# First softmax of a recurrent attention step done 320 wide, the step's end by halves, and the last step's loads put elsewhere

## The chip, the cores and the metric

The kernel runs on one core of a Trainium2 chip, as one launch. The time is the device time of that launch in microseconds (us). Five runs of the kernel before took 2143.23 to 2150.59 us, with a median of 2146.34 us.

A core has five engines that matter here: TensorE (PE, with its weight loads PEld), VectorE (DVE), ScalarE (ACT), GpSimd (POOL) and SyncE (SP, which here only issues DMAs). Each works through its own queue in order and waits on semaphores for the others. PE writes to PSUM, which has eight banks. SBUF is the working memory.

## The reference

Two independent computations stand side by side in the output. Part A is attention with a recurrent memory of 8 rows, over 64 segments of 32 rows:

```python
for s in range(n_seg):                       # 64 segments
    xs = x[:, s * seg_len:(s + 1) * seg_len, :]
    h = jnp.concatenate([mem, xs], axis=1)   # 8 + 32 rows of 1024
    q = jnp.einsum('btd,dhe->bhte', h, Wq)   # 32 heads of 128
    k = jnp.einsum('btd,dhe->bhte', h, Wk)
    v = jnp.einsum('btd,dhe->bhte', h, Wv)
    scores = jnp.einsum('bhqe,bhke->bhqk', q, k) * scale
    scores = jnp.where(mask, scores, -1e9)
    p = softmax(scores)
    o = jnp.einsum('bhqk,bhke->bhqe', p, v)
    o = jnp.einsum('bhte,hed->btd', o, Wo)
    mem = o[:, :M, :]                        # the next step's memory
    outs.append(o[:, M:, :])
```

Part B is a long convolution (a state-space kernel applied through Fourier transforms) of 2048 rows by 1024 channels. The change does not touch it.

## The kernel before

Part B comes first. Beside it, everything of part A that does not need the memory is worked out ahead: q, k and v of the last 8 rows of each segment, which are called *left rows*. Then part A runs its 64 steps, each needing the memory rows that the step before produced. After the steps, one closing product (`L607`) applies Wo to all left rows at once.

**A step** handles 32 rows: 8 memory rows and the first 24 rows of the segment (`XM = 24`). These are the *main rows*. They stand transposed in `hT` (8 tiles of 128 by 32, one for each 128 of the 1024 features). Heads go in two groups of 16, numbered 0 and 1. `quads(m, t, kcs)` (L358) makes the projections of matrix `m` and group `t` for some of the eight k tiles, four matmuls of 512 columns for each, on four quarters of the PE array. The order in a step is k0, q0, k1, q1, v0, v1, with scores, softmax and value products (`pv_x` for main rows, `pv_l` for left rows) of group 0 and then of group 1 laid between them. `oproj` (L460) applies Wo, units 0 to 7 from group 0 (`o0`), 8 to 15 from group 1 (`o1`). Its result is copied by ACT to `ob` (L565), transposed by PE and copied by DVE into `hT` (L572), and the next step's first projection can begin.

**The softmax** of a group works on a PSUM tile `sc` of 128 x 2 x 4 x 40 float32: index 0 of the second dimension holds the main rows (160 values a partition), index 1 the left rows (160 more). `highest` (L398) takes the row maxima on DVE, `below` (L401) subtracts them on DVE, `powers` (L404) takes the exponential on ACT, and `norm` (L407) sums, inverts and multiplies and transposes 32 x 32 blocks (L409 to L414), all on DVE. `spread` (L417) and `spread_l` (L421) lay the transposed weights out as block-diagonal operands of the value products, for the main rows on DVE (L419, L422); `left_blocks` (L425) does it for the left rows on POOL (L427, L422).

**The order is written out by hand**: the program's text gives each engine's queue its order. On ACT stand the copies out of PSUM (L371 `evac`, L450, L482, L507, L508, L565), the exponentials, and the DMA issues of `load_pk`, `load_vx` and `stores` (L325, L330, L342), so a DMA issue that waits holds the copies behind it. SP's queue holds the streamed weights.

**Weights.** Most of the 64 tiles of 512 KB are resident in SBUF, in places that part B has freed. Twelve are streamed from HBM in every step (`STREAM`, `STREAM_O`), through four slots in turn: `stage` (L294) puts the load on SP's queue, where it waits until PE has finished with the tile four before it. Three more are kept partly in PSUM banks and copied by DVE (`fetch`, L311) to SBUF when due.

**The arena.** The step's small tiles share 5984 bytes a partition, at the byte addresses in `AT`. Tiles that overlap wait for each other: a new tile cannot be written before the last reader of an older one in its place has finished, a store's DMA included. `ob` has two parts of 512 bytes: the first is read by the store of the output rows (L347), the second by the store of the left rows' values (L343).

**The last step** begins the closing work. `raw` are eight tiles of left-row values loaded back from HBM, `left` the same by head. POOL issues seven of the loads and makes the first eight copies `by_head`, between the first softmax and its left blocks:

```python
            for j in range(7):
                nc.gpsimd.dma_start(out=raw[j][:], in_=OLd[j])
            for j in range(4):
                for t in range(2):
                    by_head(j, t, nc.gpsimd.tensor_copy)
```

Of the kernel before, what the change touches and what calls it, by code (L numbers as in the profile page):

```python
# [35 lines left out]
AT = {"K7a": 2048, "K7b": 4960, "K7c": 0, "K7d": 3168, "ob": 1024, "pk": 3936, "vx": 0, "Q7a": 4960, "Q7b": 0, "k0": 2048,  # L36
      "q0": 4960, "KT0": 2048, "QT0": 4960, "k1": 2912, "q1": 1536, "pn0": 5664, "pt0": 1216, "ln0": 896, "lt0": 1216,
      "KT1": 1632, "QT1": 2912, "pb0": 4960, "V0": 2912, "L0": 1920, "o0": 896, "V1": 2048, "pn1": 4640, "pt1": 3072,
      "pb1": 4960, "lb1": 3392, "ln1": 4640, "lt1": 3936, "L1": 512, "o1": 4960, "Oa": 1024, "Ob": 3168}

# [192 lines left out]
def part_a(ctx, tc, x, src, WD, HE, seg_len, out_a, ahead, W_res, rest, places, first):  # L233
# [105 lines left out]
    def bc(ap, shape):  # L339
        return ap.to_broadcast(shape)  # L340
# [16 lines left out]
    for s in range(NS):  # L357
# [40 lines left out]
        def highest(sc, i):  # L398
            nc.vector.tensor_reduce(out=mx[:, 4 * i:4 * i + 4], in_=sc[:, i], axis=AX.X, op=ALU.max)  # L399

        def below(sc, i):  # L401
            nc.vector.tensor_tensor(out=sc[:, i], in0=sc[:, i], in1=bc(mx[:, 4 * i:4 * i + 4].unsqueeze(2), [128, 4, NK]), op=ALU.subtract)  # L402

        def powers(sc, i):  # L404
            nc.scalar.activation(out=sc[:, i], in_=sc[:, i], func=ACT.Exp, scale=scale)  # L405

        def norm(sc, i, pn, pt):  # L407
            m_ = mx[:, 4 * i:4 * i + 4]
            nc.vector.tensor_reduce(out=m_, in_=sc[:, i], axis=AX.X, op=ALU.add)  # L409
            nc.vector.reciprocal(out=m_, in_=m_)  # L410
            pn, pt = at(pn, 4, NK), at(pt, 5, SL)
            nc.vector.tensor_tensor(out=pn, in0=sc[:, i], in1=bc(m_.unsqueeze(2), [128, 4, NK]), op=ALU.mult)  # L412
            nc.vector.transpose(out=pt[:, 0:4, :], in_=pn[:, :, 0:SL])  # L413
            nc.vector.transpose(out=pt[:, 4:5, :], in_=pn[:, :, SL:NK])  # L414
            return pt
# [5 lines left out]
        def spread_l(eng, out, pl, j, m, n):  # L421
            eng.tensor_tensor(out=out, in0=bc(pl.unsqueeze(1), [128, m, n]),  # L422
                              in1=bc(BDL[:].rearrange("p a b -> p (a b)")[:, j:j + m].unsqueeze(2), [128, m, n]), op=ALU.mult)

        def left_blocks(lt, name):  # L425
            L = at(name, 2, 16, XL)
            nc.gpsimd.tensor_tensor(out=L[:, 0].rearrange("p (a b) k -> p a b k", a=4), in0=bc(lt[:, 0:4, 0:XL].unsqueeze(2), [128, 4, 4, XL]),  # L427
                                    in1=bc(BD[:].unsqueeze(1).unsqueeze(3), [128, 4, 4, XL]), op=ALU.mult)
            spread_l(nc.gpsimd, L[:, 1], lt[:, 4, 0:XL], 0, 16, XL)
            return L  # L430

        def pv(p, t, V, pb, lbs):
            for hl in range(4 if V is not None else 0):
                nc.tensor.matmul(p[:, hl, :], lhsT=V[:, 128 * hl:128 * hl + 128], rhs=pb[:, hl, :],  # L434
                                 start=(hl == 0), stop=False, skip_group_check=True)
            p, lo = p.rearrange("p a b -> p (a b)"), 0
            for lb in lbs:
                nc.tensor.matmul(p[:, lo:lo + lb.shape[1]], lhsT=vl[:, t, :], rhs=lb,
                                 start=False, stop=True, skip_group_check=True)
                lo += lb.shape[1]  # L440
# [12 lines left out]
        def pv_l(pl, t, V, L, parts=(0, 1)):  # L453

            if 0 in parts:
                pv(pl, t, V, L[:, 0].rearrange("p (a b) k -> p a (b k)", a=4), [])
            if 1 in parts:
                pv(pl, t, None, None, [L[:, 1].rearrange("p a k -> p (a k)")])
# [11 lines left out]
        a = quads("k", 0, range(KC))  # L470
# [10 lines left out]
        QT0, KT0 = at("QT0", 4, 4, SL), at("KT0", 4, 4, NK)  # L481
        nc.scalar.copy(out=QT0, in_=pq[:])  # L482
        vx = load_vx(s)
        nc.vector.tensor_copy(out=KT0[:, :, :, 0:SL], in_=pk_[:])  # L484
# [5 lines left out]
        highest(sc0, 0)  # L490
        below(sc0, 0)
        powers(sc0, 0)
        highest(sc0, 1)
        below(sc0, 1)
        k1 = evac(a, "k1")
        powers(sc0, 1)
        a = quads("q", 1, range(KC))
        pt0 = norm(sc0, 0, "pn0", "pt0")
        q1 = evac(a, "q1")
        sc1 = new_sc("b0")  # L500
        a = quads("v", 0, range(0, 2))
# [7 lines left out]
        if s + 1 == NS:  # L509

            spare = [W_res[m, t, kc] for m, t in (("k", 0), ("q", 0), ("k", 1), ("q", 1), ("v", 0)) for kc in range(KC) if (m, t, kc) in W_res]
            raw, left = ([spare.pop(0) for _ in range(8)] for _ in range(2))

            def by_head(j, t, copy):

                copy(out=left[2 * (j // 2) + t][:].rearrange("p (h s k) -> p h s k", h=16, s=16)[:, :, 8 * (j % 2):8 * (j % 2) + 8],
                     in_=raw[j][:].rearrange("p (s h k) -> p h s k", h=32, s=8)[:, 16 * t:16 * t + 16])
            for j in range(7):
                nc.gpsimd.dma_start(out=raw[j][:], in_=OLd[j])
            for j in range(4):  # L520
                for t in range(2):
                    by_head(j, t, nc.gpsimd.tensor_copy)

        pb0 = at("pb0", 4, 4, SL)
        spread(pb0, pt0[:, 0:4, :])
        lb0 = [pk[:, 0:384], S_[:]]
        spread_l(nc.vector, lb0[0].rearrange("p (a k) -> p a k", k=SL), pt0[:, 4, :], 0, 12, SL)
        spread_l(nc.vector, lb0[1].rearrange("p (a k) -> p a k", k=SL), pt0[:, 4, :], 12, 4, SL)
        lt0 = norm(sc0, 1, "ln0", "lt0")
        quads("v", 0, range(2, KC), a)  # L530
        scores(1, sc1, QT1, KT1)
        V0 = evac(a, "V0")
        L0 = left_blocks(lt0, "L0")
        highest(sc1, 0)
        below(sc1, 0)
        powers(sc1, 0)
        highest(sc1, 1)
        a = quads("v", 1, range(0, 4))
# [5 lines left out]
        pt1 = norm(sc1, 0, "pn1", "pt1")  # L544
# [4 lines left out]
        quads("v", 1, range(4, KC), a)  # L549
# [8 lines left out]
        lt1 = norm(sc1, 1, "ln1", "lt1")  # L558
        oproj(pp[:, 1, :], range(5, 8), o0)
        L1 = left_blocks(lt1, "L1")  # L560
# [4 lines left out]
        nc.scalar.copy(out=osb, in_=pp[:, 1, :])  # L565
        pl = ps.tile([128, 4, 32], F32, name="pl", tag="b2")
        pv_l(pl[:], 1, V1, L1, (0,))
        if s + 1 < NS:
            pt_o = ps.tile([128, 2, 4, SL], BF16, name="tro", tag="b0")
            for j in range(2):  # L570
                nc.tensor.transpose(out=pt_o[:, j, :, :].rearrange("p a b -> p (a b)"), in_=osb[:, 128 * j:128 * j + 128], identity=ident[:])
            nc.vector.tensor_copy(out=hT[:, :, XM:SL].rearrange("p (q j) r -> p j q r", j=2), in_=pt_o[:, :, :, XM:SL])  # L572
        pv_l(pl[:], 1, V1, L1, (1,))
# [21 lines left out]
    nc.gpsimd.dma_start(out=raw[7][:], in_=OLd[7])  # L595
    for j in range(4, 8):
        for t in range(2):
            by_head(j, t, nc.scalar.copy if t else nc.vector.tensor_copy)
# [915 lines left out]
```

## Time and profile before

| what | number |
|---|---|
| median of five runs | 2146.34 us (2143.23 to 2150.59) |
| the profiled execution: its own time | 2140.73 us |
| its span | 2139.0 us |
| PE busy | 1874.9 us, 88% |
| DVE busy | 1453.4 us, 68% |
| ACT busy | 1050.5 us, 49% |
| POOL busy | 403.1 us, 19% |
| copy into hT (L572) starts, first and last of 63 | 777.3 and 2036.4 us |
| DMA, 1000 to 2000 us | share 0.95, 332 GB/s |
| chain that ended last: PE, DMA, DVE | 31%, 15%, 12% |

The profile is of one execution. Times count from the start of its span. An instruction is named by its line (L402 is line 402), its engine, and what it writes and reads (`out<-in`); in brackets or behind a bar stand the idle time of the engine just before it and what ended that. "Clock" is the share of PE's full clock that was granted. The DMA share is the mean busy share of the core's 16 DMA engines.

### The profile page before, as it was taken

How to read it: one execution, taken by the hardware profiler on the slowest of the kernel's cores; microseconds unless marked ns; L12 is line 12 of the kernel's file. 1: busy time of each engine (PE TensorE's matmuls, PEld its weight loads, DVE VectorE, ACT ScalarE, POOL GpSimd, SP SyncE). 2: the span in 40 equal slices, each digit the busy share in tenths (PEclk: the TensorE clock that was granted, in tenths of full speed). 3: DMA queues.
4: the chain of work that ended last, by engine and by line, in shares of the span. 5: the costliest groups of instructions: out<-in, count | busy, mean ns of one | idle time of the engine just before them, and what ended most of it. 6: DMA issues, size and time to landing. Idle time of an engine off the chain costs nothing.

```text
span 2139.0 us, 79277 instructions
## 1 busy us (share of the span) xinstructions
PE 1874.9 (88%) x33734; PEld 1182.3 (55%) x33734; DVE 1453.4 (68%) x3736; ACT 1050.5 (49%) x1919; POOL 403.1 (19%) x786
## 2 busy tenths in 40 slices
PE   1589999977999779999999999999998999999959
PEld 1365656656888435555555555555555555555534
DVE  8589999989999246666665666666665666666630
ACT  6699999971333324444444444444444444444420
POOL 2145435452101101111111111111111111111120
PEclk9999999989999879999999999999999999999979
DMA  6767886567745899999999999999999999999960
GB/s 162 188 198 230 238 229 178 161 176 206 240 134 175 301 332 334 333 329 323 334 331 329 332 341 337 327 334 332 331 328 322 331 331 335 332 335 338 336 243 20
DMA packets 344022, 590.81 MB, mean 276 GB/s; under 512 B 108536, under 2 KB 220184, under 8 KB 341620
## 3 DMA queue, kind: packets, MB, share of 16 engines
q1 hardware_dynamic: 295864, 523.80, 72.6%
q0 software_dynamic: 11696, 37.88, 5.1%
q10 hardware_dynamic: 36108, 24.07, 4.0%
q8 instruction: 264, 4.33, 0.8%
q14 instruction: 90, 0.74, 0.1%
HBM read 530.86 MB, written 65.26 MB: 279 GB/s over the span
## 4 chain that ended last, share of the span: by engine, by line
PE 31%; DMA 15%; DVE 12%; issue 4%; ACT 2%; POOL 1%; ACTq 0%; DVEq 0%; SPq 0%; POOLq 0%
PE acc L365 17%; PE pp L467 7%; DMA wst<-WD_o 6%; DMA wst<-WD_v 4%; PE pe L607 3%; DVE arena L422 2%; DMA wst<-WD_k 2%; PE tr L376 2%; DVE a_mx L399 2%; DVE arena L412 2%; DVE sc L402 2%; ACT sc L405 1%; DVE a_mx L409 1%; DVE arena L413 1%; DMA W_o<-in_A_Wo_dram 1%
## 5 line engine op out<-in xcount | busy, mean ns | idle before, releaser
L365 PEld LDWEIGHTS <-a_hT 128*32 128x32 bf16 x12352 | 325.4, 97 | 322.1 <-issue 62.8
L365 PE MATMUL acc<-W,a_hT 128*32 128x512 bf16 x4864 | 387.2, 383 | 0.0
L371 ACT CAST arena<-acc 128x512 bf16<-128x512 f32 x384 | 225.8, 588 | 303.5 <-PE acc L365 219.9
L467 PEld LDWEIGHTS <-arena 128*32 128x32 bf16 x8256 | 216.5, 97 | 93.6 <-issue 63.3
L365 PE MATMUL acc<-wst,a_hT 128*32 128x512 bf16 x2304 | 223.0, 384 | 19.0 <-DMA wst<-WD_v 8.1
L292 DVE TENSOR_SCALAR arena<-keep 128x256 int32<-128x256 int32 (+1 forms) x512 | 175.8, 395 | 50.1 <-PE acc L365 46.8
L405 ACT ACTIVATE sc<-sc 128x160 f32<-128x160 f32 x256 | 73.7, 288 | 258.1 <-DVE sc L402 248.3
L467 PE MATMUL pp<-W_o,arena 128*32 128x256 bf16 x4608 | 169.3, 275 | 8.4 <-DMA W_o<-in_A_Wo_dram 7.9
L379 POOL COPY arena<-arena 128x128 bf16<-128x128 bf16 x128 | 37.3, 292 | 700.7 <-PE tr L376 438.5
L399 DVE TENSOR_REDUCE a_mx<-sc 128x4 f32<-128x160 f32 x256 | 80.6, 315 | 120.0 <-PE sc L394 63.4
L365 PE MATMUL acc<-MF,a_hT 128*32 128x512 bf16 x2048 | 158.6, 380 | 0.0
L167 PE MATMUL pro<-xTl,wsl 128*128 128x512 bf16 x512 | 120.0, 385 | 5.2 <-ACT xTl L111 5.2
L427 POOL TENSOR_TENSOR arena<-arena,a_BD 128x128 bf16<-128x128 bf16 x128 | 51.0, 398 | 366.3 <-DVE arena L414 340.3
L1047 PEld LDWEIGHTS <-MF 128*128 128x128 bf16 x1024 | 102.6, 100 | 30.0 <-issue 8.6
L409 DVE TENSOR_REDUCE a_mx<-sc 128x4 f32<-128x160 f32 x256 | 82.2, 321 | 50.4 <-ACT sc L405 50.4
L484 DVE COPY arena<-tr 128x512 bf16<-128x512 bf16 x64 | 27.2, 425 | 130.5 <-ACT arena L371 119.6
L413 DVE STREAM_TRANSPOSE arena<-arena 128x128 bf16<-128x128 bf16 x256 | 79.7, 311 | 46.7 <-PE pp L434 19.4
L434 PEld LDWEIGHTS <-arena 128*128 128x128 bf16 x1024 | 55.5, 97 | 94.2 <-issue 61.8
L1047 PE MATMUL hps<-KT,MF 128*128 128x256 bf16 x720 | 94.1, 283 | 14.7 <-DVE x L1222 11.6
L1279 PE MATMUL yp<-Bt,MI 128*128 128x256 bf16 x680 | 102.8, 273 | 0.8 <-ACT yb L1295 0.8
L565 ACT CAST arena<-pp 128x256 bf16<-128x256 f32 x64 | 23.8, 372 | 158.3 <-PE pp L467 158.3
L1085 ACT ACTIVATE E<-pa 128x648 bf16<-128x648 f32 x128 | 91.4, 714 | 17.7 <-PE pa L1077 14.1
(321 smaller groups left out, 4083.4 us busy)
## 6 DMA issues: line engine op xcount, KB each, us to landing
wst<-WD_v SPq DMA_DIRECT2D x256, 512.0 KB
wst<-WD_k SPq DMA_DIRECT2D x192, 512.0 KB
wst<-WD_o SPq DMA_DIRECT2D x192, 512.0 KB
wst<-WD_q SPq DMA_DIRECT2D x128, 512.0 KB
Ud<-ux POOLq DMA_DIRECT2D x16, 1024.0 KB, 5.9
uq<-Ud SPq DMA_DIRECT2D x32, 512.0 KB
wsl<-in_A_Wk_dram SPq DMA_DIRECT2D x16, 512.0 KB
wsl<-in_A_Wv_dram SPq DMA_DIRECT2D x16, 512.0 KB
```

Of the source, the lines that this page charges most:

```text
L167: nc.tensor.matmul(a[:], lhsT=w[:, kc, 128 * j:128 * j + 128], rhs=xTl[:, kc, :, :].rearrange("p s k -> p (s k)"), start=(kc == 0), stop=( ...
L292: nc.vector.tensor_scalar(out=out.bitcast(I32), in0=in_.bitcast(I32), scalar1=0, scalar2=None, op0=ALU.bitwise_or)
L365: nc.tensor.matmul(a[32 * g:32 * g + 32, o_:o_ + rhs.shape[1]], lhsT=hT[:, kc, :], rhs=rhs, start=(kc == 0), stop=(kc == KC - 1), tile_pos ...
L371: nc.scalar.copy(out=q, in_=a[:])
L399: nc.vector.tensor_reduce(out=mx[:, 4 * i:4 * i + 4], in_=sc[:, i], axis=AX.X, op=ALU.max)
L405: nc.scalar.activation(out=sc[:, i], in_=sc[:, i], func=ACT.Exp, scale=scale)
L409: nc.vector.tensor_reduce(out=m_, in_=sc[:, i], axis=AX.X, op=ALU.add)
L413: nc.vector.transpose(out=pt[:, 0:4, :], in_=pn[:, :, 0:SL])
L467: nc.tensor.matmul(po[32 * qt:32 * qt + 32, o_:o_ + rhs.shape[1]], lhsT=oT[:, h % 4, (h % 16) // 4, :], rhs=rhs, start=False, stop=(h == 3 ...
L1047: pe.matmul(s_[r][half][:, cs, :], lhsT=MF[:, kc, 4 * rr + mc, cs, :], rhs=rhs, start=(i == 0 and mc == 0), stop=(i == 1 and mc == 3), ski ...
L1085: sc.activation(out=T["E", r, e // 4][:, lo:lo + 8 * NE].rearrange("p (i c) -> p i c", i=2), in_=T.pop(("p", r, e))[:, :, 0:4 * NE], func= ...
L1279: pe.matmul(yp[:, b, :], lhsT=m_[:, b, cs, kc, :], rhs=Bt[:, kc, j, half, c_, :], start=(kc == 0 and cs == 0 and half == 0), stop=(kc == 3 ...
```

## The change

1. The first softmax of a step works on both indices of `sc0` together, 320 values a partition: one maximum, one subtraction, one exponential, one sum, one inverse, one product, and two transposes of twice the width. `flat` and `maxima` give the view. `norm` is split into `weigh` and `turn`.
2. In the second softmax the left rows' maximum moves from before the main rows' sum to after the spread `lb1`.
3. The first softmax's spreads change order: key-side first, then the main one; `left_blocks` follows them at once, ahead of the second softmax.
4. At the step's end `ob`'s rows are copied in two halves of 128 columns, transposed into two PSUM banks and copied into `hT` in two copies, the even k tiles first. The first projection takes its k tiles in the order 0, 2, 4, 6, 1, 3, 5, 7. The left-value products of group 1 are in one piece ahead of the transposes.
5. PE's queue: three k tiles of v0 instead of two before the transposes of k1 and q1; six of v1 instead of four before the first value products. On ACT the copy of k1 moves ahead of the exponential.
6. The last step loads two `raw` tiles on SP's queue; four `by_head` copies on POOL follow the left blocks. The other six loads go to SP after the output weights, their copies to DVE and POOL alternately (before: DVE and ACT).
7. All arena addresses are new.

```diff
+AT = {"K7a": 4960, "K7b": 2048, "K7c": 1024, "K7d": 3136, "ob": 3904, "pk": 0, "vx": 3392, "Q7a": 2048, "Q7b": 4960,
+      "k0": 1024, "q0": 2048, "KT0": 4704, "QT0": 1024, "k1": 1024, "q1": 4288, "pn0": 5312, "pt0": 2304, "KT1": 1024,
+      "QT1": 4288, "pb0": 4288, "V0": 1024, "L0": 5472, "o0": 2368, "V1": 1024, "pn1": 2048, "pt1": 4288, "pb1": 0,
+      "lb1": 4960, "ln1": 320, "lt1": 0, "L1": 2048, "o1": 3904, "Oa": 4960, "Ob": 2560}
...
+        def flat(sc, i):
+            return sc[:].rearrange("p i h k -> p (i h) k") if i is None else sc[:, i]
+
+        def maxima(i):
+            return mx[:, 0:8] if i is None else mx[:, 4 * i:4 * i + 4]
 
         def below(sc, i):
-            nc.vector.tensor_tensor(out=sc[:, i], in0=sc[:, i], in1=bc(mx[:, 4 * i:4 * i + 4].unsqueeze(2), [128, 4, NK]), op=ALU.subtract)
+            x, m_ = flat(sc, i), maxima(i)
+            nc.vector.tensor_reduce(out=m_, in_=x, axis=AX.X, op=ALU.max)
+            nc.vector.tensor_tensor(out=x, in0=x, in1=bc(m_.unsqueeze(2), [128, x.shape[1], NK]), op=ALU.subtract)
...
+        def weigh(sc, i, pn):
+            x, m_ = flat(sc, i), maxima(i)
+            nc.vector.tensor_reduce(out=m_, in_=x, axis=AX.X, op=ALU.add)
             nc.vector.reciprocal(out=m_, in_=m_)
...
+            pn = at(pn, x.shape[1], NK)
+            nc.vector.tensor_tensor(out=pn, in0=x, in1=bc(m_.unsqueeze(2), [128, x.shape[1], NK]), op=ALU.mult)
+            return pn
+
+        def turn(pn, pt):
+            n = pn.shape[1]
+            pt = at(pt, n + n // 4, SL)
+            nc.vector.transpose(out=pt[:, 0:n, :], in_=pn[:, :, 0:SL])
+            nc.vector.transpose(out=pt[:, n:n + n // 4, :], in_=pn[:, :, SL:NK])
             return pt
...
-        a = quads("k", 0, range(KC))
+        a = quads("k", 0, (0, 2, 4, 6, 1, 3, 5, 7))
...
-        highest(sc0, 0)
-        below(sc0, 0)
-        powers(sc0, 0)
-        highest(sc0, 1)
-        below(sc0, 1)
         k1 = evac(a, "k1")
-        powers(sc0, 1)
+        below(sc0, None)
+        powers(sc0, None)
         a = quads("q", 1, range(KC))
-        pt0 = norm(sc0, 0, "pn0", "pt0")
+        pt0 = turn(weigh(sc0, None, "pn0"), "pt0")
         q1 = evac(a, "q1")
         sc1 = new_sc("b0")
-        a = quads("v", 0, range(0, 2))
+        a = quads("v", 0, range(0, 3))
...
-            for j in range(7):
-                nc.gpsimd.dma_start(out=raw[j][:], in_=OLd[j])
-            for j in range(4):
+            for j in range(2):
+                nc.sync.dma_start(out=raw[j][:], in_=OLd[j])
+
+        quads("v", 0, range(3, KC), a)
+        scores(1, sc1, QT1, KT1)
...
+        pb0 = at("pb0", 4, 4, SL)
+        spread(pb0, pt0[:, 0:4, :])
+        L0 = left_blocks(pt0[:, 4:8, :], pt0[:, 9, :], "L0")
+        if s + 1 == NS:
+            for j in range(2):
                 for t in range(2):
                     by_head(j, t, nc.gpsimd.tensor_copy)
...
         V0 = evac(a, "V0")
-        L0 = left_blocks(lt0, "L0")
-        highest(sc1, 0)
         below(sc1, 0)
         powers(sc1, 0)
-        highest(sc1, 1)
-        a = quads("v", 1, range(0, 4))
+        a = quads("v", 1, range(0, 6))
...
-        nc.scalar.copy(out=osb, in_=pp[:, 1, :])
+        for j in range(2):
+            nc.scalar.copy(out=osb[:, 128 * j:128 * j + 128], in_=pp[:, 1, 128 * j:128 * j + 128])
         pl = ps.tile([128, 4, 32], F32, name="pl", tag="b2")
-        pv_l(pl[:], 1, V1, L1, (0,))
+        pv_l(pl[:], 1, V1, L1)
         if s + 1 < NS:
-            pt_o = ps.tile([128, 2, 4, SL], BF16, name="tro", tag="b0")
+            pt_o = [ps.tile([128, 4, SL], BF16, name="tro", tag=tag) for tag in ("b0", "b1")]
             for j in range(2):
-                nc.tensor.transpose(out=pt_o[:, j, :, :].rearrange("p a b -> p (a b)"), in_=osb[:, 128 * j:128 * j + 128], identity=ident[:])
-            nc.vector.tensor_copy(out=hT[:, :, XM:SL].rearrange("p (q j) r -> p j q r", j=2), in_=pt_o[:, :, :, XM:SL])
-        pv_l(pl[:], 1, V1, L1, (1,))
+                nc.tensor.transpose(out=pt_o[j][:].rearrange("p a b -> p (a b)"), in_=osb[:, 128 * j:128 * j + 128], identity=ident[:])
+            for j in range(2):
+                nc.vector.tensor_copy(out=hT[:, :, XM:SL].rearrange("p (q j) r -> p j q r", j=2)[:, j], in_=pt_o[j][:, :, XM:SL])
...
     stores(NS - 1, ob)
-    nc.gpsimd.dma_start(out=raw[7][:], in_=OLd[7])
-    for j in range(4, 8):
+    for j in range(2, 8):
+        nc.sync.dma_start(out=raw[j][:], in_=OLd[j])
+    for j in range(2, 8):
         for t in range(2):
-            by_head(j, t, nc.scalar.copy if t else nc.vector.tensor_copy)
+            by_head(j, t, nc.vector.tensor_copy if t else nc.gpsimd.tensor_copy)
```

## The prediction

> **What bounds the kernel now.** I read the page's 40 slices first, then one long window, then the chain of waits of two steps, then the timeline of the last step.
>
> ```profile
> PE   1589999977999779999999999999998999999959
> PEclk9999999989999879999999999999999999999979
> DMA  6767886567745899999999999999999999999960
> L365 PE MATMUL acc<-wst,a_hT 128*32 128x512 bf16 x2304 | 223.0, 384 | 19.0 <-DMA wst<-WD_v 8.1
> ```
> The recurrence fills the slices from the fifteenth on. There PE and the DMA engines are both at nine tenths. In the last slice but one PE falls to 5 tenths with the DMA engines at 6: that is the last step. The memory copy of the step end (line 572) starts first at 777.3 us and last at 2036.4 us, 62 steps apart, so a step takes 20.31 us.
>
> ```profile
> 1000.00:2000.00 1000.00, 931.49 (x20978) 543.92 (x20966) 626.50 (x2218) 436.52 (x985) 120.63 (x345) 1.00 0.95 332
> ```
> The columns are PE, weight load, DVE, ACT, POOL, clock, DMA share, GB/s. A DMA share of 0.95 is 19.3 us of every step. A step cannot get much under that, however short its chain becomes.
>
> ```profile
> 1454.72 0.34 DVE a_mx L399
> ...
> 1459.43 0.25 DVE a_mx L409
> ...
> 1460.67 0.22 DVE a_mx L399
> ...
> 1463.65 0.69 DVE arena L422
> 1464.35 0.04 issue
> 1464.39 0.38 PE pv L438
> 1464.77 2.68 PE pp L467 x86
> ...
> 1467.53 0.38 ACT arena L565
> ...
> 1468.28 0.20 DVE a_hT L572
> ```
> This is one step without a weight wait: line 572 is at 1448.40 and again at 1468.28, so 19.88 us. The other 0.43 us of 20.31 is waiting for streamed tiles; the page agrees (19.0 in the row above and 8.4 for the output weights, over 64 steps). From the first scores (1454.72) to the second value product (1464.39) the chain is DVE's queue, almost without a gap, and PE waits at its end. After that it is output projection, ACT's copy, transposes, DVE's copy into hT.
>
> ```profile
> 2062.47 3.98 POOL L516 COPY W<-Wlow 128x1024 bf16<-128x1024 bf16 x4
> ...
> 2070.36 0.39 POOL L427 TENSOR_TENSOR arena<-arena,a_BD 128x128 bf16<-128x128 bf16 x1
> 2070.80 0.27 PE L434 MATMUL pp<-arena 128*128 128x32 bf16 x4 [21.15 <-POOL arena L427]
> ```
> In the last step POOL issues seven loads and makes eight copies ahead of the left blocks L0 (line 427), and PE stands for 21.15 us.
>
> **The last step.** Its projections begin at 2036.65 and its output projection's last matmul at 2078.32: 41.7 us. In the step above the same stretch is 1448.65 to about 1467.2, 18.6 us. The excess of 23.1 us is the stall and, after it, PE at half rate (the granted clock is 0.50 in 2056 to 2070 and 0.74 in the next 10 us). The change takes the seven loads off POOL's queue, and puts only four copies (1.03 us each, line 516) behind L0. They lie between L0 and L1: POOL's two groups at line 427 start at 1440.25 and 1445.89, 5.6 us apart, and 0.8 for L0 plus 4.1 fits. Uncovered they would hold L1 by up to 4.1. The two loads move to SP's queue, ahead of a value tile: 1 MB at 332 GB/s is 3.2 us of transfers before the tiles of that step. I take 1.6, half, since tiles now land with some slack; bounds 0 and 8 (both loads and all copies uncovered). Gain 21.5, from 15 to 23.1. The six later loads, on SP behind the output weights, and twelve copies (six POOL, 6.2 us; six DVE at 0.42, 2.5 us) lie under the first quarter of the closing product (2078.64 to 2092.45, 13.8 us), which needs only tiles 0 and 1. Without that cover they cost 6.2.
>
> **First softmax, 320 wide.** Line 402 takes 0.331 us for 160 values and the 512-wide DVE cast of line 612 0.69, so 1.02 ns a value and 0.49 for 320. ACT: 0.288 (line 405) and 0.588 for 512 (line 371) give 0.42; the 320-wide mask copy has 0.43. Transposes: 0.311 and 0.169 for 128 and 32 columns give 0.50 and 0.22 for 256 and 64. The new chain from 1454.72: reduce 0.49, subtract 0.49, handover 0.11, exponential 0.42, back 0.03, sum 0.49, reciprocal 0.18, product 0.49, transposes 0.65, gaps 0.15; together 3.50, ending at 1458.22. The key-side spreads (line 422, 0.55 + 0.28) wait for POOL's copy of the left keys, which ends at 1458.30, and are done by 1459.1. The main spread (0.42) now stands behind the second scores: its place in the arena is QT1's, so a new DVE wait. These scores start when ACT has copied QT1; ACT gets to it 0.1 earlier than before as no exponential stands ahead of q1's copy. They are visible at 1459.36, so the second softmax starts at about 1459.70 instead of 1460.60. It is shorter by one maximum (0.24 of the queue): the end of lb1 moves from 1464.34 to 1463.20, 1.14 earlier.
>
> That maximum is only moved: it now stands after lb1, ahead of the subtraction and the exponential, and ACT's copy of o1 is queued behind that exponential, with output projection 8 to 15 behind it. lb1 to o1's copy was 0.48 (1464.34 to 1464.82) and becomes 0.83. Left: 0.79.
>
> **PE's moved pieces.** A third value tile before the k1/q1 transposes fills 0.21 us in which PE waited for ACT. Six v1 tiles before the value products instead of four add 0.43 before them; PE then reaches the second value product at about 1463.0, before lb1. Cost nothing; if lb1 came earlier, up to 0.4. Joining the five left-value products hides under ACT's 0.37 copy (0.07 if not). The order of the KT0 and QT0 copies is on two engines: nothing.
>
> **Step end by halves.** Now: copy 0.38, two transposes, copy 0.19, first matmul 1.00 after the start (1467.53 to 1468.53). By halves: 0.27 (line 576, 128 wide), handover 0.06, transpose 0.22, copy 0.16, handovers 0.09: 0.80. The second half runs 0.17 behind and is wanted only from the fifth k tile, 0.85 later. Gain 0.20; 0 if the first matmul waits for both.
>
> **What is late next.** Chain gain: 0.79 + 0.20 = 0.99 a step. Three things take from it.
> *POOL beside DVE.* L0 comes right after the transposes, so POOL's two products (0.40 each) run beside DVE's spreads.
>
> ```profile
> 1646.92 0.68 DVE L422 TENSOR_TENSOR arena<-arena,a_BDL 128x512 bf16<-128x512 bf16 x1
> 1647.03 0.77 POOL L337 COPY a_hT<-arena 128x192 bf16<-128x192 bf16 x1 [2.31 <-PE acc L365]
> ```
> This copy takes 0.343 alone and 0.77 here. The other way round line 419, 0.425 alone, has a maximum of 0.604, and line 422 one of 0.829. Bounds 0 and 0.50; I take 0.30, since the main spread waits anyway. The Trainium skill, "SBUF — State Buffer", section "Who interferes with whom", says that a DVE instruction with two SBUF inputs and a GpSimd instruction reading SBUF exclude each other for a whole instruction. By that rule the two products and the spreads run one after another and the loss would be 0.50, the forecast 2110.
> *Stores.* The new place of ob overlaps that of vx and KT0. So ACT's load of vx (4.9 us into the step) waits for the store of the rows, with k1's copy and the exponential behind it on ACT, and KT0's copy waits for the other store. In the trace's semaphore updates the row store lands 5.75 us into the step at the median, 7.6 at the ninth decile, 9.6 at most; the other 4.2 and 5.2. The chain is late only by what the landing exceeds 6.6 (6.6 + 0.33 issue + 0.59 copy + 0.42 exponential, less the slack before the main spread). Bounds 0 and 0.45; I take 0.15, the mean over these deciles, less what weight waits cover.
> *Weights.* 19.3 us of DMA in a step of some 19.8 would be a share of 0.97, above any 100 us window I read (0.96). I add 0.10 to the 0.43; bounds 0 and 1.0.
> Net 0.99 - 0.30 - 0.15 - 0.10 = 0.44 a step, 63 steps: 27.7 us.
>
> **Sum.** 27.7 + 21.5 = 49.2 us. The profiled execution has a span of 2139.0 and a time of 2140.73, 1.7 outside; it lies 5.6 below the median of the runs, so I take the saving from the median: 2146.3 - 49.2 = 2097.
>
> **Rivals.** (1) The weights take back the steps. For it: DMA at 0.95 now, and waits in steps of up to 1.7 us. Against: many steps run at 19.88 with no weight wait. Only the last step gains: 2146.3 - 21.5 = 2125. (2) Neither POOL nor the stores cost anything: 0.89 x 63 + 21.5 = 77.6, so 2069. For it: the median landing is before 6.6. (3) Slower: the row store holds ACT at vx's load. If busier DMA engines make it land at 9.6 in every step, the chain is 3.0 late: 63 x 3.0 - 63 x 0.99 - 21.5 = 105, so 2251. It decides from a mean landing of about 7.9. Against: today's median is 5.75. (4) Another stall in the last step, loads late or the four copies ahead of L1, 11 us: 2108.
>
> **How the numbers follow.** Forecast 0.45, rival 1 0.22, rival 2 0.20, rival 3 0.05, rival 4 0.06, no change at all 0.02. The range takes in rivals 1 and 2: 2066 to 2126. Within 0.2% (4.3 us) a measurement of this kernel cannot tell a change from none. Faster 0.93, same 0.02, slower 0.05.
>
> **What would show it.** Right: no PE wait over 3 us in the last step and a clock of 1.0 up to the closing product; DVE rows of about 0.49 at 320 wide; the distance of the hT copies near 19.9; DMA share 0.96 to 0.98. Wrong: ACT idle ahead of vx's load or k1's copy with the row store as releaser; spreads of lines 419 and 422's successors well over 0.43 and 0.55; first k matmul waiting for the second half; PE waiting for streamed tiles by over 0.6 us a step.

## The result and the profile after

The changed kernel takes 2139.55 us in the median, where the kernel before takes 2142.95 in the same set of runs. The ratio is 0.9977 (95% interval 0.9968 to 0.9987): faster by 0.23%, some 5 us. 49 were forecast. Below, a ratio is turned into microseconds with 2143.

The page of the profiled execution (span 2132.3 us), three of its slice rows and the row that answers to the one shown of before:

```profile
PE   1589999977999779999989999999999999999999
PEclk9999999988999879999999999999999999999999
DMA  6767886566745899999999999999999999999991
L365 PE MATMUL acc<-wst,a_hT 128*32 128x512 bf16 x2304 | 233.7, 384 | 45.7 <-DMA wst<-WD_v 35.7
```

The dent in the last slice but one is gone: PE and its clock stay at nine tenths to the end. But PE's idle time ahead of streamed tiles, 19.0 us before, is 45.7, and what was added is put down to W_v (8.1 before, 35.7 now).

The same stretch of 1000 us as before, in the columns PE, weight load, DVE, ACT, POOL, clock, DMA share, GB/s:

```profile
1000.00:2000.00 1000.00, 926.37 (x20646) 535.57 (x20635) 605.50 (x1891) 431.94 (x974) 145.60 (x340) 1.00 0.94 327
```

PE makes fewer instructions in it (20646 for 20978), and the DMA share is lower. The steps have become longer, not shorter. The copies into hT (now L575, two a step) say by how much: the first half's copy ends at 773.0 in the first of 63 steps and at 2051.4 in the last, 62 steps apart, so a step takes 20.62 us where it took 20.31.

The waits view of PE alone shows what became of its idle time in these 1000 us. The columns are total, times and longest; gaps under 0.15 us are not listed. Before:

```profile
PE tro L571 <- ACT arena L565: 18.5, 49, 0.7
PE acc L365 <- DVE a_hT L572: 11.4, 50, 0.2
PE pp L434 <- POOL arena L427: 7.1, 28, 0.3
PE acc L365 <- DMA wst<-WD_v: 6.4, 15, 1.5
PE pp L467 <- DMA wst<-WD_o: 6.1, 14, 1.2
```

After:

```profile
PE acc L365 <- DMA wst<-WD_v: 21.5, 41, 1.6
PE tro L573 <- ACT arena L567: 8.7, 45, 0.2
PE pp L474 <- DMA wst<-WD_o: 8.6, 15, 1.4
PE tr L376 <- ACT arena L371: 8.1, 13, 1.5
PE sc L390 <- DVE arena L489: 5.2, 7, 1.5
PE pp L474 <- ACT arena L460: 3.3, 14, 0.3
...
PE acc L365 <- DVE a_hT L575: 0.9, 3, 0.4
```

What the change was to shorten did shorten: the two waits of the step's end went from 29.9 to 9.6, and the wait for POOL's left blocks is gone. In their place stand the W_v tiles (41 waits in some 48 steps) and two waits that the kernel before hardly had: for ACT's copy ahead of the k1 and q1 transposes, and for DVE's copy of KT0.

The last step, from the timeline of the changed kernel, in which the stall of 21.15 us stood:

```profile
2062.18 4.17 POOL L519 COPY W<-Wlow 128x1024 bf16<-128x1024 bf16 x4
2063.04 0.40 PE L365 MATMUL acc<-wst,a_hT 128*32 128x512 bf16 x4 [1.59 <-DMA wst<-WD_v]
...
2072.32 2.75 PE L610 MATMUL pe<-W,W 128*128 128x512 bf16 x12
```

POOL's four copies lie beside PE's work, and the longest wait left is 1.59 us, for a streamed tile queued behind the two raw loads. From the last copy into hT to the closing product is now 20.9 us; it was 42.0. So the last step gave back 21 us, and the 62 steps before it took most of that away.

How the steps lose time shows in one of the longest, the step from 1020.66 to 1042.69 (22.02 us, with no wait for a weight tile). Its timeline:

```profile
1021.07 0.57 ACTq L347 DMA_DIRECT2D out_dram<-arena  x1
...
1025.81 0.42 DVE L489 COPY arena<-tr 128x512 bf16<-128x512 bf16 x1 [2.36 <-DMA OLd<-arena]
...
1030.02 0.33 ACTq L333 DMA_DIRECT2D arena<-VXd  x1
1030.44 0.59 ACT L371 CAST arena<-acc 128x512 bf16<-128x512 f32 x1 [4.26 <-DMA out_dram<-arena]
1030.92 0.43 ACT L410 ACTIVATE sc<-sc 128x320 f32<-128x320 f32 x1
1031.08 0.40 PE L376 MATMUL tr<-a_ident,arena 128*128 128x128 bf16 x4 [1.48 <-ACT arena L371]
```

The store of the rows is issued at 1021.07. The load of vx, whose place ob shares, cannot be issued before that store has landed, 8.95 us later. Behind it in ACT's queue stand k1's copy and the exponential, and PE waits. Worked out from the issue times of all steps: vx's load is issued 4.99 us into an undisturbed step, at 6.13 in the median, after 7.1 in 13 of 62 steps and after 8.4 in eight. Those eight take 21.5 us on average, the others 20.5.

### The profile page after: what moved, and what is told of

It is laid out like the page before. It is cut to its first block, busy times and chain, and to the rows that moved or that the text cites. A ratio compares the mean times of both kernels' runs of the same rounds, so it can differ in the third digit from the quotient of the medians.

```text
span 2132.3 us, 78633 instructions
## 1 busy us (share of the span) xinstructions
PE 1882.3 (88%) x33734; PEld 1182.8 (55%) x33734; DVE 1437.9 (67%) x3353; ACT 1046.6 (49%) x1915; POOL 437.3 (21%) x780
## 5 line engine op out<-in xcount | busy, mean ns | idle before, releaser
L365 PEld LDWEIGHTS <-a_hT 128*32 128x32 bf16 x12352 | 337.4, 96 | 334.8 <-issue 87.3
L371 ACT CAST arena<-acc 128x512 bf16<-128x512 f32 x384 | 224.8, 585 | 415.8 <-PE acc L365 277.1
L365 PE MATMUL acc<-W,a_hT 128*32 128x512 bf16 x4864 | 375.8, 383 | 0.0
L365 PE MATMUL acc<-wst,a_hT 128*32 128x512 bf16 x2304 | 233.7, 384 | 45.7 <-DMA wst<-WD_v 35.7
L474 PEld LDWEIGHTS <-arena 128*32 128x32 bf16 x8256 | 210.1, 97 | 106.7 <-ACT arena L460 52.9
L414 DVE TENSOR_REDUCE a_mx<-sc 128x4 f32<-128x160 f32 (+1 forms) x192 | 73.1, 381 | 111.0 <-ACT sc L410 111.0
L489 DVE COPY arena<-tr 128x512 bf16<-128x512 bf16 x64 | 27.2, 425 | 142.9 <-PE tr L376 102.8
L460 ACT CAST arena<-pv 128x512 bf16<-128x512 f32 x128 | 75.1, 587 | 96.1 <-PE pp L444 71.2
L437 POOL TENSOR_TENSOR arena<-arena,a_BD 128x128 bf16<-128x128 bf16 x128 | 72.4, 565 | 215.0 <-DVE arena L424 202.5
L406 DVE TENSOR_REDUCE a_mx<-sc 128x4 f32<-128x160 f32 (+1 forms) x192 | 71.9, 375 | 59.6 <-PE sc L394 58.6
L410 ACT ACTIVATE sc<-sc 128x160 f32<-128x160 f32 (+1 forms) x192 | 64.1, 334 | 94.6 <-DVE sc L407 89.0
L567 ACT CAST arena<-pp 128x128 bf16<-128x128 f32 x128 | 27.8, 269 | 160.0 <-PE pp L474 160.0
```

The lines of the kernel that those rows point to most:

```text
L365: nc.tensor.matmul(a[32 * g:32 * g + 32, o_:o_ + rhs.shape[1]], lhsT=hT[:, kc, :], rhs=rhs, start=(kc == 0), stop=(kc == KC - 1), tile_pos ...
L371: nc.scalar.copy(out=q, in_=a[:])
L406: nc.vector.tensor_reduce(out=m_, in_=x, axis=AX.X, op=ALU.max)
L414: nc.vector.tensor_reduce(out=m_, in_=x, axis=AX.X, op=ALU.add)
L460: nc.scalar.copy(out=o, in_=p[:].rearrange("p a (g q) -> p a g q", g=4))
L474: nc.tensor.matmul(po[32 * qt:32 * qt + 32, o_:o_ + rhs.shape[1]], lhsT=oT[:, h % 4, (h % 16) // 4, :], rhs=rhs, start=False, stop=(h == 3 ...
```

## The experiments

Two theories at the outset. A: the new places make ACT and DVE wait for store landings. B: the streamed tiles set the pace, by one tile that is now wanted too early (B1) or by a full queue (B2). Most kernels below are the changed kernel with one thing altered; "step" is the mean distance of the hT copies unless it is called median, and the undisturbed steps of a kernel are the shortest ones, which agree within 0.02 us in the kernels with nine tiles. Where the line that holds `AT` is shorter, numbers are three lower (L368 is L371 of the changed kernel).

**1. Other places.**

```diff
-"vx": 3392, "q0": 2048, "KT0": 4704, "QT0": 1024, "q1": 4288, "pn0": 5312, "pt0": 2304, "QT1": 4288, "pb0": 4288,
-"L0": 5472, "o0": 2368, "pt1": 4288, "lb1": 4960, "ln1": 320, "lt1": 0, "Oa": 4960
+"vx": 4928, "q0": 2304, "KT0": 1024, "QT0": 2304, "q1": 3904, "pn0": 2304, "pt0": 3264, "QT1": 3904, "pb0": 3904,
+"L0": 2368, "o0": 2880, "pt1": 2368, "lb1": 3904, "ln1": 0, "lt1": 5440, "Oa": 0
```

> The changed kernel with the places in the arena dealt anew, so that the row output ob no longer lies under anything that the next step writes in its first 12 us (vx and KT0 leave it; the first to reuse it is q1). No instruction is added, dropped or moved. Theory A (the steps lost time to the store landings: 8 of 62 steps have vx's load held until the row store has landed and take 21.6 us where the others take 20.4; 9 have KT0's copy held by the OLd store and take 20.9): some 8 x 1.2 + 9 x 0.4 = 13 us less than the changed kernel, ratio to the kernel before near 0.992, no ACT idle time put down to out_dram, the second wait for OLd gone from DVE. Theory B (streamed weights alone set the pace; a step that a store delays gives its tiles time that they need anyway): within 4 us of the changed kernel, ratio 0.996 to 0.998, and PE's waits for wst grow by as much as the store waits shrink.

Measured: 0.9874 (0.9845 to 0.9902), that is 22 us less than the changed kernel; step 20.20. From its waits view:

```profile
PE acc L362 <- DMA wst<-WD_v: 20.7, 46, 1.4
...
ACT arena L368 <- DMA out_dram<-arena: 14.5, 11, 2.1
...
PE tr L373 <- ACT arena L368: 3.7, 7, 1.0
```

Theory A, and more of it than expected (22 for 13). PE's wait for DVE's KT0 copy is gone and the one for ACT is halved; together that is 9.6 us in 1000, 0.20 a step, so the rows name only part of the 22 us. W_v's is as it was, so it isn't a shadow of the store waits. One expectation missed: some ACT waits for the row store stay, since q1 lies under ob here.

**2. The order of W_v(1).**

```diff
-        a = quads("v", 1, range(0, 6))
+        a = quads("v", 1, (0, 1, 2, 3, 4, 6))
...
-        quads("v", 1, range(6, KC), a)
+        quads("v", 1, (5, 7), a)
```

> The changed kernel with one order changed: of the six W_v(1) tiles ahead of the first value product the streamed tile 5 is replaced by the kept tile 6, and 5 comes after the product with 7. The places stay those of the changed kernel. Theory B1 (the changed kernel asks for tile v1,5 at 12.0 us in the step, and it lands at 12.9 in the median because its slot came free with q1,4 at 7.5: 0.32 us of wait a step in 38 of 59 steps, where the kernel before asked at 13.3 and waited 0.00): 0.2 to 0.3 us a step less, 12 to 20 us, ratio to the kernel before 0.988 to 0.992, wst waits back at 0.45 a step. Theory B2 (the queue as a whole is full, DMA busy 0.94 of the step): the wait moves on to the o tiles, 0 to 4 us less, ratio 0.996 to 0.998.

Measured: 0.9945 (0.9919 to 0.9970), 7 us less than the changed kernel.

```profile
PE pp L474 <- DMA wst<-WD_o: 13.9, 29, 1.1
...
PE acc L365 <- DMA wst<-WD_v: 6.5, 16, 1.5
```

Between the two theories by the time, and the intervals leave room for either; the rows tell more. The W_v wait falls from 21.5 to 6.5, as before the change; a third of it comes back at the output tiles.

**3. Both.**

> Both edits together. Theory (two separate waits): the gains add, 25 to 33 us less than the changed kernel, ratio to the kernel before 0.983 to 0.987, steps near 20.1. If both only give time back to a full queue: not over 8 us less than the changed kernel, ratio over 0.994, DMA share of the step above 0.96.

Measured: 0.9814 (0.9788 to 0.9840), 2106.92 us, 35 less than the changed kernel. The gains add (22 and 7 alone), and the interval lies below those of both kernels of the case. Its steps take 20.11, still far from the shortest, which take 19.24.

**4. The last step alone**, on the kernel before.

```diff
-            for j in range(7):
-                nc.gpsimd.dma_start(out=raw[j][:], in_=OLd[j])
-            for j in range(4):
-                for t in range(2):
-                    by_head(j, t, nc.gpsimd.tensor_copy)
+            for j in range(2):
+                nc.sync.dma_start(out=raw[j][:], in_=OLd[j])
...
         L0 = left_blocks(lt0, "L0")
+        if s + 1 == NS:
+            for j in range(2):
+                for t in range(2):
+                    by_head(j, t, nc.gpsimd.tensor_copy)
...
```

> The kernel before with the last step's part of the change alone: two raw left tiles ahead of the closing product, on SP's queue, their four copies on GpSimd behind L0, the other six tiles after the loop, their copies by GpSimd and VectorE. The prediction's step: 21.5 us less than before (15 to 23.1), ratio 0.990 (0.989 to 0.993). If the stall only changes its releaser (the raw loads late, or the closing product waiting for its tiles): under 8 us less, ratio over 0.996.

Measured: 0.9913 (0.9884 to 0.9942), 19 us (12 to 25). The stall of 21.15 us is gone; the longest wait left in the last step is 2.8 us, for a W_v tile.

**5 to 8. Nine streamed tiles instead of twelve**, to see the steps with the queue unloaded (the DMA share of the 1000 us is 0.75 to 0.76). In `unit`:

```diff
+        if key in WD and key[0] == "o":
+            return unit(("o", 0))
         if key in rest:
```

> The kernel before with nine streamed tiles a step instead of twelve: the output units 1, 5 and 9 are computed with the resident tile of unit 0 in their place, so the steps' output projection is not the reference's, and 1.5 MB a step less is moved; everything else is as it was. It shows what the steps take when the streamed tiles are never late. Theory (the step's floor is 19.88 us, the rest is weight waits of 0.43): 27 us less than before, ratio 0.987, hT copies 19.9 apart, wst waits under 0.05 a step. If the waits stem from single late tiles whatever the load: ratio over 0.995.

Measured: 0.9867 (0.9842 to 0.9893), 28.5 us less than before. More than half of the steps take 19.87 or 19.88. The expected 0.05 for weight waits missed: 0.23 us a step remains, bunched in some of the steps.

> The changed kernel with the same nine streamed tiles (units 1, 5 and 9 computed with unit 0's tile). Theory A (store landings and weights both grow with the load on the DMA engines): stores land sooner, few are waited for, steps of 19.3 to 19.6, 35 to 60 us below the nine-tile kernel before, ratio 0.958 to 0.970. Rival (the store waits come from the places alone and cost the same with a free queue): steps of 19.7 to 19.9, ratio 0.971 to 0.978.

Measured: 0.9709 (0.9689 to 0.9729), 34 us below e5_before_9; step 19.80. By its number it sits in the rival's range, but not for the rival's reason. ACT's waits for the row store are down to 1.6 us in 1000, from 31.9, so the store waits did come from the load on the DMA engines together with the places. What stays is this, PE's first row:

```profile
PE acc L367 <- DMA wst<-WD_v: 23.1, 38, 1.5
```

So tile 5 of W_v(1) is late even with a quarter of the traffic gone: it makes 36 of the 51 W_v waits of the 62 steps, 0.34 us a step (0.32 in the changed kernel). Its load waits for the slot of the tile four before it and is issued 7.53 us into the step, PE wants it at 12.0, and in the steps that wait it lands 4.8 to 6.8 us after its issue. B1, a matter of order more than of load.

> The kernel with the new places and the v1 order (e3_places_v1), with the same nine streamed tiles. Theory C (an undisturbed step went from 19.88 to 19.23: PE had 1.08 us of idle time a step to give, 0.48 at the value products and 0.60 at the step's end, and 0.42 is left): 0.65 x 63 + 21 = 62 us below the nine-tile kernel before, ratio to the kernel before 0.958, steps of 19.2 to 19.3. The prediction's step (0.99 a step if neither POOL nor stores nor weights take any of it): 0.99 x 63 + 21 = 83, ratio 0.948, steps of 18.9. If the steps' gain was never there: ratio 0.975 or more.

Measured: 0.9636 (0.9612 to 0.9659), 49.5 us below e5_before_9. The median step is 19.26, as theory C had it; the mean is 19.56, since some steps still wait for a tile, so the steps gain 0.47 in the mean and the whole stays under theory C's 62 us. PE's waits in 1000 us of e5_before_9:

```profile
PE tro L573 <- ACT arena L567: 18.8, 50, 0.7
...
PE acc L367 <- DVE a_hT L574: 11.4, 50, 0.2
PE pp L436 <- POOL arena L429: 8.0, 32, 0.3
```

and of e7_mended_9:

```profile
PE pp L473 <- ACT arena L459: 6.0, 33, 0.3
PE tro L572 <- ACT arena L566: 3.3, 21, 0.2
...
PE acc L364 <- DVE a_hT L574: 0.6, 3, 0.2
```

This is what the chain part of the change is worth where nothing else interferes: 19.88 to 19.24 in the undisturbed steps, 0.64.

For e8_mended_9_whole the end of the step is as before, apart from the left-value product, which stays in one piece:

```diff
-        for j in range(2):
-            nc.scalar.copy(out=osb[:, 128 * j:128 * j + 128], in_=pp[:, 1, 128 * j:128 * j + 128])
+        nc.scalar.copy(out=osb, in_=pp[:, 1, :])
...
-        a = quads("k", 0, (0, 2, 4, 6, 1, 3, 5, 7))
+        a = quads("k", 0, range(KC))
```

> e7_mended_9 with the step's end by halves undone: one copy of 256 columns, both transposes into one bank, one copy into hT, k tiles in the order 0 to 7. Theory C (the halves took PE's idle time at the step's end from 0.60 to 0.25): 0.35 x 63 = 22 us more than e7_mended_9, steps of 19.55 to 19.6. The prediction's step (0.20): 13 us more. If the first matmul waited for both halves: no difference.

Measured: 0.9684 (0.9657 to 0.9711), 10 us more than e7_mended_9; undisturbed steps 19.42. The prediction's 0.20 was right (0.18), theory C's 0.35 was not:

```profile
PE acc L364 <- DVE a_hT L572: 14.5, 51, 0.3
PE tro L571 <- ACT arena L565: 12.7, 49, 0.3
```

PE's two waits here make 27.2, close to the 30.2 of e5_before_9, and 3.9 by halves. Part of that fall is only that the gaps by halves are too short for the view. With the short ones PE stands at the end of an undisturbed step for 0.54 us here and 0.25 by halves: 0.29 less, for a step 0.18 shorter. So idle time read off one place is no exact measure of the gain.

**9. Two tiles later.**

```diff
-quads("v", 1, (0, 1, 2, 3, 4, 6))
+quads("v", 1, (0, 2, 3, 4, 1, 6))
...
-oproj(pp[:, 1, :], range(8, 16), o1)
+oproj(pp[:, 1, :], (8, 10, 11, 9, 12, 13, 14, 15), o1)
```

> e3_places_v1 (twelve streamed tiles, places and v1 order mended) with two more streamed tiles used later within their own product: W_v(1) goes 0, 2, 3, 4, 1, 6 and the output units 8, 10, 11, 9, 12 to 15. In e3_places_v1 the two have the largest waits (0.16 and 0.10 us a step of 0.47). If each wait belongs to its tile: 0.15 to 0.25 us a step less, 10 to 16 us, ratio to the kernel before 0.974 to 0.977. If the queue as a whole is full (DMA busy 19.3 of 20.1 us a step): the waits move to the tiles behind, ratio 0.980 to 0.983.

Measured: 0.9817 (0.9787 to 0.9846), no change against e3_places_v1. The W_v wait falls and the output tiles take it over, in PE's rows:

```profile
PE pp L471 <- DMA wst<-WD_o: 20.0, 42, 1.5
...
PE acc L362 <- DMA wst<-WD_v: 4.6, 14, 0.8
```

With tile 5 out of the way, this fits B2 at twelve tiles.

**10. The first softmax narrow again**, in the mended kernel with nine tiles.

```diff
-        below(sc0, None)
-        powers(sc0, None)
+        for i in range(2):
+            below(sc0, i)
+            powers(sc0, i)
...
-        pt0 = turn(weigh(sc0, None, "pn0"), "pt0")
+        pn0, pt0 = at("pn0", 8, NK), at("pt0", 10, SL)
+        for i in range(2):
+            x_, m_, h_ = flat(sc0, i), maxima(i), slice(4 * i, 4 * i + 4)
+            nc.vector.tensor_reduce(out=m_, in_=x_, axis=AX.X, op=ALU.add)
+            nc.vector.reciprocal(out=m_, in_=m_)
+            nc.vector.tensor_tensor(out=pn0[:, h_], in0=x_, in1=bc(m_.unsqueeze(2), [128, 4, NK]), op=ALU.mult)
+            nc.vector.transpose(out=pt0[:, h_, :], in_=pn0[:, h_, 0:SL])
+            nc.vector.transpose(out=pt0[:, 8 + i:9 + i, :], in_=pn0[:, h_, SL:NK])
```

> e7_mended_9 (nine streamed tiles) with the first softmax 160 wide again, twice, in the changed order otherwise: maximum, subtraction and exponential of the main rows, then of the left rows; sum, inverse, product and transposes likewise. By rows, four passes cost 2 x 0.33 for 0.49, the inverse 0.18 more, the transposes 0.31 more: 1.17 us more of DVE before the second softmax. Theory C (the wide softmax gives PE only the 0.4 to 0.5 us that it waited at the value products, but this order without it runs over that): 0.7 to 1.1 a step more than e7_mended_9, 45 to 70 us, ratio 0.985 to 0.996. Rival (the gain at the value products came from the order of the queues and the sixth v1 tile, not from the width): under 0.2 a step, ratio 0.964 to 0.970.

Measured: 0.9854 (0.9828 to 0.9880), 47 us more than e7_mended_9; median step 20.24, 0.99 longer. Theory C. The width is what makes the new order pay: with narrow passes this order is slower than the order before (20.24 for 19.88).

```profile
PE pp L473 <- ACT arena L459: 17.6, 72, 0.5
...
PE pv L443 <- DVE arena L428: 6.5, 33, 0.3
```

PE now waits for the spreads, and for o0 and o1.

**11. No GpSimd work beside the spreads.**

```diff
-        L0 = left_blocks(pt0[:, 4:8, :], pt0[:, 9, :], "L0")
+        L0 = left_blocks(pt0[:, 4:8, :], pt0[:, 9, :], "L0") if s == 0 else at("L0", 2, 16, XL)
```

> e7_mended_9 with GpSimd's two products for L0 made in the first step alone; later steps read what lies in L0's place, so the left rows' values of group 0 are not computed. VectorE's key-side spreads then have no GpSimd work beside them. The prediction's step (POOL beside DVE costs 0.30 a step): 19 us less than e7_mended_9, ratio 0.955. Theory C (the spreads take 0.45 longer, but the main spread behind them waits for the second scores anyway, and no PE wait follows): within 4 us of e7_mended_9, ratio 0.962 to 0.966, and DVE idle ahead of the main spread instead.

Measured: 0.9619 (0.9593 to 0.9644), 4 us below e7_mended_9, within the two intervals; mean step 19.54 for 19.56. The main spread starts 10.92 us into the step in the median of both kernels. Groups of DVE by form: count, busy, mean ns, idle before. e7_mended_9, then e11_no_L0_9:

```profile
L428 DVE TENSOR_TENSOR arena<-arena,a_BDx 128x512 bf16<-128x512 bf16 x102 | 44.9, 440 | 4.3 <-issue 1.8
L431 DVE TENSOR_TENSOR arena<-arena,a_BDL 128x384 bf16<-128x384 bf16 x51 | 40.8, 799 | 6.4 <-POOL arena L378 2.2
...
L431 DVE TENSOR_TENSOR a_S<-arena,a_BDL 128x128 bf16<-128x128 bf16 x51 | 24.6, 483 | 0.0
```

```profile
L428 DVE TENSOR_TENSOR arena<-arena,a_BDx 128x512 bf16<-128x512 bf16 x103 | 45.6, 442 | 25.8 <-ACT arena L510 25.0 <-issue 0.7
...
L431 DVE TENSOR_TENSOR arena<-arena,a_BDL 128x384 bf16<-128x384 bf16 x51 | 29.2, 572 | 6.4 <-POOL arena L378 2.2
L431 DVE TENSOR_TENSOR a_S<-arena,a_BDL 128x128 bf16<-128x128 bf16 x51 | 15.4, 302 | 0.0
```

The key-side spreads are 0.23 and 0.18 us shorter without GpSimd, and the main spread behind them waits that much longer for the second scores (idle 25.8 us in 51 steps for 4.3, put down to L510, ACT's copy of QT1, which these scores read). The interference is real and costs nothing here.

**12. q1 out of ob's place too.**

```diff
-"vx": 4928, "q1": 3904, "pn0": 2304, "pt0": 3264, "QT1": 3904, "pb0": 3904, "L0": 2368, "o0": 2880,
-"lb1": 3904, "lt1": 5440, "o1": 3904, "Ob": 2560
+"vx": 5088, "q1": 2048, "pn0": 3072, "pt0": 4448, "QT1": 2304, "pb0": 2368, "L0": 3392, "o0": 3904,
+"lb1": 2880, "lt1": 5600, "o1": 2880, "Ob": 3904
```

> e3_places_v1 with the places dealt once more, so that q1 leaves ob's place too: ob now lies under nothing that the next step writes before pt0, and under pt0 only with the part that the OLd store reads. In e3_places_v1 ACT still stands 13.8 us (9 times) for the row store and 20.2 us (9 times) for the OLd store in 1000 us, and PE 5.7 us (6 times, 2.6 at most) for ACT's copies of k1 and q1 ahead of their transposes. Theory A (what is left of the store landings costs time as well): 4 to 10 us less than e3_places_v1, ratio to the kernel before 0.977 to 0.980, ACT's waits for out_dram gone. Rival (a step that no store holds waits for its streamed tiles instead): within 3 us, ratio 0.980 to 0.983, PE's waits for wst up by the same.

Measured: 0.9838 (0.9812 to 0.9864); step 20.11, the same as e3_places_v1. Its waits:

```profile
PE pp L471 <- DMA wst<-WD_o: 14.0, 26, 1.2
PE acc L362 <- DMA wst<-WD_v: 11.3, 22, 1.2
```

In e3_places_v1 these two rows are:

```profile
PE acc L362 <- DMA wst<-WD_v: 8.6, 13, 1.4
PE pp L471 <- DMA wst<-WD_o: 7.4, 13, 1.5
```

The rival, just above its range, which the interval reaches into. ACT's waits for the row store are gone, and the time goes to the streamed tiles.

## Why the prediction failed, step by step

Forecast and measurement, in us a step, gains positive:

| step of the sum | forecast | measured | from |
|---|---|---|---|
| chain up to the value products, with PE's moved pieces | +0.79 | +0.46 | undisturbed steps, e5 to e8: 19.88 to 19.42 |
| step's end by halves | +0.20 | +0.18 | e8 to e7: 19.42 to 19.24 |
| POOL beside DVE | -0.30 | 0.00 | e11 |
| stores | -0.15 | -0.35 | e1: 22 us over 63 steps, all that other places gave |
| tile 5 of W_v(1) wanted earlier | none | -0.11 to -0.20 | e2; e1 to e3 |
| other waits for streamed tiles | -0.10 | -0.31 to -0.40 | what is left of the sum, not all of it tile waits (below) |
| steps together | +0.44 | -0.22 | changed kernel against e4: 0.0064 x 2143 / 63 |
| last step (once, us) | +21.5 | +19 to 21 | e4; the distance in the profile |

An interval of 0.0025 on a ratio is 0.09 us a step, so the second digit of these is not certain; by the trace the steps lost 0.31.

**Right.** The last step, with its details: no wait over 3 us, a clock of 1.00 up to the closing product, raw loads that cost 1.6 (1.59 in the trace; half of 3.2 was a guess, so this match is partly luck), POOL's copies covered, and the closing product as long as before (60.0 us for 60.4). The rows at 320 wide: 0.49 to 0.50 for each of the passes on DVE, 0.43 for the exponential, 0.45 and 0.20 for the transposes. The halves: the first matmul does not wait for the second half. Two of the signs named for "wrong" came true and point at the cause: ACT idle ahead of k1's copy with the row store as releaser, and streamed tiles waited for by 0.73 us a step over the 62 steps. A third, longer spreads, came true and cost nothing. Two of the signs for "right" failed: the distance of the hT copies (20.62 for 19.9) and the DMA share (0.94).

**"Left: 0.79" was read from the wrong engine.** DVE's chain did move: in undisturbed steps the end of lb1 went from 15.74 us into the step to 14.78, 0.96 against 1.14 forecast. But the sum booked that movement as time, though PE, which sets the step, did not wait that long for it. In the step of the kernel before that the prediction read, PE's rows at the value products are these:

```profile
1461.20 0.25 PE L434 MATMUL pp<-arena 128*128 128x32 bf16 x4 [0.25 <-POOL arena L427]
1461.56 0.22 PE L438 MATMUL pp<-arena 128*128 128x128 bf16 x1
...
1463.88 0.38 PE L434 MATMUL pv<-arena 128*128 128x128 bf16 x4
1464.39 0.38 PE L438 MATMUL pv<-arena 128*128 128x512 bf16 x1
```

From each row's end to the next, and in the bracket, its idle time is 0.25 + 0.11 + 0.13 = 0.49 us. No more could be had there, and the later copy of o1 takes 0.17 of it back. That is 0.32 of the 0.46; PE's idle time at the step's end is 0.06 less in e8_mended_9_whole than in e5_before_9, and the last 0.08 lies in no gap of PE. The chain of waits runs through DVE because the last 0.13 us hang on it, not because 1.14 do. From e5_before_9 to e7_mended_9 all gaps of PE in an undisturbed step fall from 1.11 to 0.45 us, 0.67 for a step that is 0.64 shorter.

**POOL beside DVE**: both ends of the bound were reasonable, the value was not. The prediction itself said that the main spread waits for the second scores. In undisturbed steps of e7_mended_9 the spreads, longer by 0.41 us in all, end at 10.86 and the main spread starts at 10.92, so they were covered, and the term came out at nothing. The rule of the Trainium skill that was weighed ("SBUF — State Buffer", "Who interferes with whom") shows in the rows in part: 0.57 to 0.80 and 0.30 to 0.48. The first of these spreads starts together with a GpSimd product of 0.40 us and is 0.23 longer, so the loss is less than a whole instruction. The price of 0.50 by that rule would have been wrong too.

**Stores**: the mechanism was right, down to vx's load, ACT's queue and k1's copy, and the size was off: 0.35 for 0.15, within its bound of 0.45. The term was worked out from landings in the kernel before, and only from what exceeds 6.6 us. In the changed kernel vx's load is issued later than 7.1 us into 13 of 62 steps, 6.2 to 8.9 us after the store. KT0's copy, which the term left at nothing, makes PE wait too, 5.2 us in 1000. The 0.35 is all that the other places gave, and PE's rows name 0.20 of it. Rival 3 was this mechanism in every step; it came in one of five.

**Weights**: two terms in one. For tile 5 the prediction asked what six W_v(1) tiles cost PE, and not whether the sixth had landed. That was readable: a tile four slots back is only just freed. The rest was taken as 0.10 on the ground that a DMA share of 0.97 had not been seen; in fact the share over 1000 us never rose above 0.96 and the steps stayed longer instead. In PE's rows over the 62 steps the waits for tiles other than tile 5 do grow by 0.10 a step (0.31 before, 0.41 after; the prediction had read 0.43 for before, from page rows that include a wait of 4.0 us at 723 us, in the first step). So what is left of the sum is only in part waits for tiles. Another 0.15 is in PE's time outside any gap, 18.92 us a step before and 19.07 after, and 18.8 in the kernels e5 to e8 with nine tiles. Once the stores and tile 5 are mended, e3_places_v1 gains 0.34 a step over e4_last_step, of the 0.64 that are there; with nine tiles the mean gain is 0.47. e9_tiles_later and e12_q1_clear moved waits about and did not get the rest back.

Rival 1 (the steps' gain given back) came nearest, and the outcome went beyond it. The range ended where the steps gain nothing. The bounds of stores and weights, 0.45 and 1.0, together exceed the chain's gain, so it had to reach past that point.

**What stays open**: why single W_v tiles come late by up to 1.4 us at a DMA share of 0.75 (e5_before_9, in 15 waits over 1000 us). Over the 62 steps 17 of its 20 waits are for tile 1 of W_v(1). Its load is issued 5.27 us into the step and PE wants it at 10.96, so the ring of four slots gives it 5.7 us; in these 17 steps it took 6.1 to 7.7. No run here tells what delays it then, nor why PE's time outside its gaps is longer with twelve tiles.

## What to carry to other kernels

Price a shortened chain at no more than about the idle time of the engine that sets the pace, in its own rows and with the short gaps, and not by how far the chain's end moves. When buffers get new addresses, list for each new overlap who the last reader is; where it is a store, the next writer waits for a landing whose tail, not its median, decides, and a DMA issue that waits holds everything behind it in its queue. When work with streamed operands is moved forward, compare each tile's landing (the release of its slot plus the time from issue to landing) with the time at which it is now wanted.

## What was unexpected in the hardware

A store of 64 KB took 6.2 to 8.9 us from issue to the release of its reader's place in the 13 steps that it held, under a DMA share of 0.94. With a quarter of the streamed traffic gone (share 0.76), ACT's waits for the row store fell from 31.9 us in 1000 to 1.6, and by the semaphore updates the store landed 3.7 us after its issue in the median and 4.6 at the ninth decile, where it took 5.4 and 7.7: the landing's tail belongs to the load. GpSimd suffers beside VectorE too: its 128-wide product of L431 takes 557 ns on average over L0 and L1 in e7_mended_9, which is 714 for L0, beside the spreads, and 399 for L1.
